# Moving the value loads of a cached attention kernel from SyncE's queue to GpSimd's

## The chip, the cores and the metric

One core of a Trainium2 chip runs the whole program. Its time is the device time of one execution in microseconds (us); the median of two executions before the change is 1309.85 us (1309.16 and 1310.54). The engines named below are PE (TensorE), DVE (VectorE), ACT (ScalarE), POOL (GpSimd) and SP (SyncE). Loads from memory are carried by 16 DMA engines; an engine such as SP or POOL only issues them.

## The reference

Four sequences (B = 4) decode one token each. Attention has 32 heads of width 128 over a cache of 4096 keys and values; beside it stands a gated feed-forward part of width 1792; a gate mixes the two. All data are float32.

```python
def _A_ref(x, k_cache, v_cache, wq, wo):
    q = (x @ wq).reshape(B, Sq, H, Dh).transpose(0, 2, 1, 3)
    scores = jnp.einsum("bhqd,bhkd->bhqk", q, k_cache) * (Dh ** -0.5)
    p = _softmax(scores, axis=-1)
    o = jnp.einsum("bhqk,bhkd->bhqd", p, v_cache)
    return o.transpose(0, 2, 1, 3).reshape(B, Sq, H * Dh) @ wo

def _B_ref(x, w_gate, w_up, w_down):
    return (_gelu(x @ w_gate) * (x @ w_up)) @ w_down

g = _sigmoid((x * gate_w).sum(-1, keepdims=True))
return g * _A_ref(x, k_cache, v_cache, wq, wo) + (1 - g) * _B_ref(x, w_gate, w_up, w_down)
```

The two caches are 268 MB each and are read once. That is nearly all the data that the program moves.

## The kernel before

The work on the caches is cut into NT = 32 tiles: tile i holds the keys (or the values) of four heads of one sequence. In SBUF a tile is 128 partitions by 16384 elements, so 64 KB in each partition and 8.39 MB in all. Partition (h, p) holds 128 consecutive positions of head h.

For tile i, DVE multiplies the keys by the query (`products`, L379) and sums over the head width (`sums`, L385). It does so in two pieces, 32 of the 128 positions first (or last), which it calls shared, then the other 96. Then `soft_max` finds the maximum (L390 to L392), and ACT computes the weights into the one tile PM (L397). PE multiplies the values by the weights (`pv`, L411, 64 matmuls). Each second tile ACT copies the result (`gather_a`, L419), and each fourth tile PE and DVE collect it (`gather`, `weigh`).

One tensor, `big`, holds the large data. It has room for two K tiles which overlap by a quarter (that is why 32 positions of each tile are called shared: their place is needed by the next K tile), and behind them for one V tile. So the load of K tile i + 1 can start once DVE has summed the shared quarter of tile i, and the load of V tile i once PE has finished `pv(i - 1)`. The last V tile goes to the place of K tiles, which is free sooner. The weights use the same space: wq, w_gate and w_up lie in the V place before V tile 0, w_down and wo lie in the K and V places after the tiles that stood there.

The order of the instructions of each engine is the order in which the plan's steps are added in the program; nothing is reordered later. `Plan.add` works out, from the places that a step reads and writes, for which earlier steps it has to wait. Each step counts in a lane, which becomes a semaphore. Compute steps count in their engine's own lane. A load counts in the lane that it names, by 16, and the loads that share a lane have to be in one order. PE, DVE and ACT run the regular turns in a loop over k; the loads aren't in a loop but are written out one by one, each with its wait, in the stream of the issuing engine.

Before the change all loads are issued by SP, through `load` (L255): wq, x, gate_w and K tile 0 at the start, then w_gate and w_up, K tile 1, V tile 0, and from there K and V in turn, at the end w_down and eight pieces of wo. Lanes: "k" for K tiles and also for w_down, "v" for V tiles and for one piece of wo, "vl" for the last V tile, others for the weights. POOL builds the identity matrix at the start (L293, L294) and waits for SP at the very end, to clear the semaphores.

Of the kernel before, what the change touches and what calls it, by code (L numbers as in the profile page):

```python
# [19 lines left out]
class Plan:  # L20
# [18 lines left out]
    def add(self, engine, emit, reads=(), writes=(), lane=None, unit=1):  # L39
        lane = lane or engine  # L40
        self.units[lane] = unit
        row = self.by_lane.setdefault(lane, [])
        step = Step(lane, engine, emit, self.turn if engine in self.loops else None)
        step.at = len(row)
        need = {}
        for accesses, writing in ((reads, False), (writes, True)):
            for name, lo, hi in accesses:
                for other, a, b, wrote in self.past.get(name, ()):
                    if a < hi and lo < b and (wrote or writing):
                        if other.lane == engine and engine == "pe":  # L50
                            continue
                        if other.lane == engine and not wrote:
                            continue
                        need[other.lane] = max(need.get(other.lane, -1), other.at)
        seen = self.seen[engine]
        for l, n in sorted(need.items(), key=lambda x: -len(self.by_lane[x[0]])):
            if seen.get(l, -1) >= n:
                continue
            other = self.by_lane[l][n]
            other.asked = True  # L60
            step.waits[l] = n
            seen[l] = n
            for k, v in self.knew[other].items():
                seen[k] = max(seen.get(k, -1), v)
        step.waits = {l: n for l, n in step.waits.items()
                      if not any(self.knew[self.by_lane[m][k]].get(l, -1) >= n for m, k in step.waits.items() if m != l)}
        self.knew[step] = dict(seen)
        self.knew[step][lane] = step.at
        if row and lane == engine:
            for k, v in self.knew[row[-1]].items():  # L70
                if k != lane:
                    self.knew[step][k] = max(self.knew[step].get(k, -1), v)
        for accesses, writing in ((reads, False), (writes, True)):
            for name, lo, hi in accesses:
                old = self.past.get(name, [])
                if writing:
                    old = [x for x in old if not (lo <= x[1] and x[2] <= hi)]
                self.past[name] = old + [(step, lo, hi, writing)]
        row.append(step)
        self.steps.append(step)  # L80
        return step
# [51 lines left out]
def tile_gated_mix(tc: tile.TileContext, x, kc, vc, wq, wo, w_gate, w_up, w_down, gate_w, out):  # L133
    nc = tc.nc
    P = 128
    B, H, S, D = kc.shape
    DM = x.shape[2]
# [7 lines left out]
    NT = B * NG  # L145
    TW = R * D
# [4 lines left out]
    FC = F // P  # L151
# [15 lines left out]
    def sb(pool, name, shape):  # L167
        sizes[name] = math.prod(shape[1:])
        return pool(name, [P] + list(shape[1:]), F32).ap()[:shape[0]]
# [37 lines left out]
    q = sb(ps, "q", [P, B, D])  # L207
# [6 lines left out]
    Q0, F0, F1, W0, D0 = VA, VA, VA + KC * F, VA, VA + TW // 2  # L214
# [4 lines left out]
    def place(a, n):  # L219
        return big[:, a:a + n]  # L220

    def z(a, n):
        return ("big", a, a + n)
# [15 lines left out]
    add = plan.add  # L239
# [14 lines left out]
    def load(dst, src, writes, lane):  # L254
        return add("sp", lambda: nc.sync.dma_start(dst, src), (), writes, lane=lane, unit=16)  # L255

    def load_kv(kind, i):
        src = (vc, kc)[kind == "k"]
        a = KB_ * (i % 2) if kind == "k" else VA if i < NT - 1 else 0
        s = src[i % B, HT * (i // B):HT * (i // B) + HT].rearrange("h (p r) d -> (h p) (r d)", p=PH)  # L260
        load(place(a, TW), s, [z(a, TW)], "vl" if kind == "v" and i == NT - 1 else kind)

    def KA(i):
        return KB_ * (i % 2)
# [6 lines left out]
             [z((F0, F1)[s], KC * F)], f"f{s}")  # L271

    def load_d():
        load(place(D0, FC * DM), w_down.rearrange("(p i) n -> p (i n)", i=FC), [z(D0, FC * DM)], "k")

    def load_w(w):
        src = wo[w * HW * D:(w + 1) * HW * D].rearrange("(p e) n -> p (e n)", e=E)
        for n, (e0, e1) in enumerate(zip(WO_END[w], WO_END[w][1:])):
            a, m = (W0, W1)[w] + e0 * DM, (e1 - e0) * DM
            lane = (("q",), ("f0", "f1", "g", "v", "x", "w"))[w][n]  # L280
            if (w, e1) == (1, E):
                for lane, b in ((lane, 0), ("e", DM // 2)):
                    load(place(a + b, DM // 2), src[:, e0 * DM + b:e0 * DM + b + DM // 2], [z(a + b, DM // 2)], lane)
            else:
                load(place(a, m), src[:, e0 * DM:e1 * DM], [z(a, m)], lane)

    load(place(Q0, KC * H * D), wq.rearrange("(p c) n -> p (c n)", c=KC), [z(Q0, KC * H * D)], "q")
    load(x_sb, x.rearrange("b s d -> (b s) d"), [z(XS, DM)], "x")
    load(gw, gate_w.rearrange("(s n) -> s n", s=1).to_broadcast([B, DM]), [z(GS, DM)], "g")
    load_kv("k", 0)  # L290
    opening = len(plan.steps)

# [185 lines left out]
    def attended(w, e):  # L478
        a, m = ES + w * E * 32 + e * 32, (W0, W1)[w] + e * DM
        return place(a, 32), place(m, DM), [z(a, 32), z(m, DM)]  # L480
# [55 lines left out]
    for i in range(NT):  # L536
        g, b = divmod(i, B)
# [5 lines left out]
        if i < NT - 1:  # L543
            load_kv("k", i + 1)
        else:
            load_kv("v", i)
# [19 lines left out]
        if i > 0 and b == 0:  # L566
            weigh(g - 1)
    plan.turn = None
    load_d()
    load_w(0)  # L570
    load_w(1)
    expand(0)
    pv(NT - 1)
# [19 lines left out]
    s, w, reads = attended(1, E - 1)  # L593
# [51 lines left out]
```

## Time and profile before

| | |
|---|---|
| median of 2 executions | 1309.85 us |
| the profiled execution's own time | 1309.37 us |
| span of its profile | 1308.0 us |
| moved by DMA | 564.81 MB, mean 432 GB/s |
| busy: DVE | 1155.1 us (88%) |
| busy: PE, weight loads | 352.0 us (27%), 100.0 us (8%) |
| busy: ACT, POOL | 87.3 us (7%), 0.7 us |
| median from issue to landing, K tiles and V tiles | 29.7 us, 29.4 us |

A row of the profile that stands for a group of instructions names line, engine, operation, output and inputs with shapes, how often it occurs, then its busy time, the mean of one, and the idle time of the engine just before, with what ended it. A row of the timeline begins with start and duration in us; in brackets stand the idle time before it and its releaser. A load's row (SPq) shows only the issue on SP; when the data landed is seen from the instruction that waited for it. A row of waits gives the sum, the number and the longest of the waits of one line for one cause. A row of windows gives start and end, length, busy time and number of instructions of PE, weight loads, DVE, ACT and POOL, the clock granted to TensorE, the mean busy share of the DMA engines and GB/s.

### The profile page before, as it was taken

To read this page: it belongs to the slowest core of one execution; us is meant where nothing else is said; L and a number is where in the kernel's file an instruction comes from. 1 tells how busy PE (TensorE), PEld (TensorE's weight loads), DVE (VectorE), ACT (ScalarE), POOL (GpSimd) and SP (SyncE) were. 2 spreads that over 40 slices of the span, in tenths; PEclk is the share of its full clock that TensorE was granted. 3 is DMA by queue.
4 is the path that set the end of the run, shared out by engine and by line. 5 is a ranking of instruction groups with operands and counts; after the bars stand their busy time and mean duration, and the time that the engine had idled before them with its cause. 6 is when DMAs were issued, how large, how long until landed. Compare 5 with 4: busy or idle time off the path is not lost.

```text
span 1308.0 us, 6147 instructions
## 1 busy us (share of the span) xinstructions
PE 352.0 (27%) x2504; PEld 100.0 (8%) x2504; DVE 1155.1 (88%) x299; ACT 87.3 (7%) x291; POOL 0.7 (0%) x6
## 2 busy tenths in 40 slices
PE   2302233202333211322321233321133222122227
PEld 0100001000010000100000000100001000010003
DVE  1899999999899998989989898998989899898991
ACT  0000000000000000000000000000000000000001
POOL 0000000000000000000000000000000000000000
PEclk9656666556666656666656666665667665566669
DMA  9999999999999999999999999999999999999998
GB/s 417 419 443 425 441 441 423 443 429 439 427 441 425 441 427 439 435 433 441 429 439 429 441 425 441 425 441 429 439 439 427 443 429 439 427 441 425 439 428 370
DMA packets 10977, 564.81 MB, mean 432 GB/s; under 512 B 1228, under 2 KB 1484, under 8 KB 1880
## 3 DMA queue, kind: packets, MB, share of 16 engines
q1 hardware_dynamic: 10968, 564.69, 99.7%
q8 instruction: 6, 0.10, 0.0%
q14 instruction: 3, 0.02, 0.0%
HBM read 564.67 MB, written 0.01 MB: 432 GB/s over the span
## 4 chain that ended last, share of the span: by engine, by line
DMA 71%; DVE 28%; issue 1%; PE 0%; SPq 0%; ACT 0%; DVEq 0%; POOLq 0%
DMA big<-in_A_k_cache 69%; DVE big L379 14%; DVE sc L385 13%; DMA big<-in_A_wo 2%; SPq L255 0%; PE acc L493 0%; PE wide L485 0%; DVE hT L525 0%; DVE m L390 0%; DVE big L523 0%; DVE big L522 0%; DVE big L520 0%; ACT big L499 0%; ACT big L521 0%; DVE res L602 0%
## 5 line engine op out<-in xcount | busy, mean ns | idle before, releaser
L379 DVE TENSOR_TENSOR big<-big,qb 128x4096 f32<-128x4096 f32 x64 | 555.9, 8686 | 88.2 <-DMA big<-in_A_k_cache 88.2
L385 DVE TENSOR_REDUCE sc<-big 128x32 f32<-128x4096 f32 x64 | 555.9, 8686 | 2.3
L411 PE MATMUL po<-big,PM 128*32 128x512 f32 x2048 | 293.7, 738 | 902.5 <-DMA big<-in_A_v_cache 902.5
L411 PEld LDWEIGHTS po<-big,PM 128*32 128x32 f32 x2048 | 72.3, 132 | 1117.5 <-DMA big<-in_A_v_cache 826.7
L397 ACT ACTIVATE PM<-sc,nb 32x128 f32<-32x128 f32 x128 | 67.2, 525 | 476.2 <-DVE nb L392 429.5
L419 ACT ACTIVATE o<-po 128x512 f32<-128x512 f32 x16 | 9.6, 597 | 448.7 <-PE po L411 448.7
L397 ACT ACTIVATION_READ_ACCUMULATOR PM<-sc,nb 32x1 f32 x128 | 26.1, 204 | 0.0
L369 ACT ACTIVATE qb<-q 128x512 f32<-128x512 f32 x8 | 4.8, 597 | 247.9 <-PE q L367 247.9
L428 PE MATMUL sm<-o,sel 128*16 128x128 f32 x128 | 15.4, 273 | 5.1 <-ACT o L419 5.1
L312 DVE COPY xT<-sg 128x128 f32<-128x128 f32 x4 | 0.9, 282 | 17.9 <-PE sg L307 17.9
L506 PE MATMUL q<-big,xT 128*32 128x448 f32 x64 | 9.9, 784 | 14.4 <-DMA big<-in_B_w_gate 11.2
L428 PEld LDWEIGHTS sm<-o,sel 128*16 128x16 f32 x128 | 11.7, 97 | 12.8 <-ACT o L419 11.4
L602 DVE COPY res<-acc 4x128 f32<-4x128 f32 x1 | 0.3, 279 | 13.5 <-PE acc L493 13.5
L461 DVE TENSOR_TENSOR tm<-oT,gmask 128x256 f32<-128x256 f32 x2 | 0.8, 424 | 12.6 <-PE oT L455 12.6
L367 PE MATMUL q<-QM,hc 128*128 128x512 f32 x16 | 9.4, 667 | 4.2 <-DVE hc L363 4.2
L390 DVE TENSOR_REDUCE m<-sc 128x1 f32<-128x128 f32 x32 | 9.2, 286 | 1.1
L325 PE MATMUL po<-big,xT 128*32 128x512 f32 x64 | 8.7, 701 | 1.0 <-DVE xT L312 1.0
L391 DVE STREAM_TRANSPOSE mt<-m 128x32 f32<-128x32 f32 x32 | 6.8, 212 | 1.1
L485 PE MATMUL wide<-big 128*32 128x512 f32 x54 | 6.6, 597 | 2.8 <-DMA big<-in_A_wo 2.8
L392 DVE TENSOR_REDUCE nb<-mt 128x1 f32<-128x32 f32 x32 | 5.9, 186 | 1.1
L307 PE MATMUL sg<-ident,big 4*128 4x4 f32 x4 | 0.6, 254 | 23.2 <-DMA big<-in_A_x 23.2
L342 DVE TENSOR_TENSOR big<-po,amask 128x512 f32<-128x512 f32 x2 | 1.3, 684 | 5.9 <-PE po L325 5.9
(72 smaller groups left out, 58.3 us busy)
## 6 DMA issues: line engine op xcount, KB each, us to landing
big<-in_A_wo SPq DMA_DIRECT2D x1, 4096.0 KB, 27.3
big<-in_B_w_gate SPq DMA_DIRECT2D x1, 3584.0 KB, 17.2
big<-in_B_w_up SPq DMA_DIRECT2D x1, 3584.0 KB, 25.4
big<-in_B_w_down SPq DMA_DIRECT2D x1, 3584.0 KB, 18.1
big<-in_A_wo SPq DMA_DIRECT2D x2, 1024.0 KB, 25.8
big<-in_A_wo SPq DMA_DIRECT2D x2, 768.0 KB, 29.5
big<-in_A_k_cache SPq DMA_DIRECT2D x32, 29.7
big<-in_A_v_cache SPq DMA_DIRECT2D x32, 29.4
```

The lines of the kernel that those rows point to most:

```text
L325: last = T.matmul(PO[s][32 * j:32 * j + 32].rearrange("p j d -> p (j d)"), xTf[:, c, :32], w[:, n0:n0 + HB * D], start=c == 0, stop=c == K ...
L367: pe(lambda: T.matmul(q.rearrange("p b d -> p (b d)"), HC.rearrange("p h k -> p (h k)"), QM.rearrange("p b d -> p (b d)"), start=True, sto ...
L379: dve(lambda: V.tensor_tensor(k, k, QB[:, b:b + 1, :].to_broadcast([P, r1 - r0, D]), op=OP.mult), m + t("qb"), m)
L385: dve(lambda: V.tensor_reduce(SC[i % 2][:, r0:r1], k, axis=AX.X, op=OP.add), [z(KA(i) + r0 * D, (r1 - r0) * D)], [(f"sc{i % 2}", r0, r1)])
L390: dve(lambda: V.tensor_reduce(M1[n], SC[n], axis=AX.X, op=OP.max), t(f"sc{n}"), t(f"m1{n}"))
L391: dve(lambda: V.transpose(MT, M1[n].to_broadcast([P, PH])), t(f"m1{n}"), t("mt"))
L397: last = A.activation(PM[:, PZ:].rearrange("p (c m) -> p c m", m=32)[s, :, h:RJ * HT:HT], SC[n][s, :].rearrange("p (c j) -> p c j", j=RJ), ...
L411: last = T.matmul(PO[n][32 * c:32 * c + 32].rearrange("p j d -> p (j d)"), PM[:, m0:m0 + 32], place(VAT(i) + j * N, N), start=b == 0 and j ...
L419: act(lambda: A.activation(O[n], PO[n], AF.Copy), t(f"po{n}"), t(f"o{n}"))
L428: T.matmul(sm[:B * HT, :D], selv[:, j, m0:m0 + B * HT], O[n][:, j, :], start=(n, j) == (0, 0), stop=(n, j) == (N - 1, RJ - 1))
L485: pe(lambda: T.matmul(wide[32 * c:32 * c + 32, :], s, w, start=n < 4, stop=n >= NW - 4), reads, t("wide"))
L506: last = T.matmul(q.rearrange("p b d -> p (b d)")[32 * j:32 * j + 32, :FG], xTf[:, c, :32], place((F0, F1)[s] + c * F + j * FG, FG), start ...
```

## The change

All V tiles are issued by POOL (`nc.gpsimd.dma_start`) in place of SP, in their old order and with the waits that the plan works out for them on POOL. K tiles and all weights remain with SP. Since loads of two issuing engines can't share a lane's count here, w_down moves from lane "k" to a lane "d" of its own, and the piece of wo that counted in "v" counts in a new lane "w2". Places in SBUF, sizes of the loads and the work of all compute engines are as before.

```diff
@@ -258,7 +258,10 @@
         src = (vc, kc)[kind == "k"]
         a = KB_ * (i % 2) if kind == "k" else VA if i < NT - 1 else 0
         s = src[i % B, HT * (i // B):HT * (i // B) + HT].rearrange("h (p r) d -> (h p) (r d)", p=PH)
-        load(place(a, TW), s, [z(a, TW)], "vl" if kind == "v" and i == NT - 1 else kind)
+        if kind == "v":
+            add("pool", lambda: nc.gpsimd.dma_start(place(a, TW), s), (), [z(a, TW)], lane="vl" if i == NT - 1 else "v", unit=16)
+        else:
+            load(place(a, TW), s, [z(a, TW)], kind)
@@ -271,13 +274,13 @@
     def load_d():
-        load(place(D0, FC * DM), w_down.rearrange("(p i) n -> p (i n)", i=FC), [z(D0, FC * DM)], "k")
+        load(place(D0, FC * DM), w_down.rearrange("(p i) n -> p (i n)", i=FC), [z(D0, FC * DM)], "d")
 
     def load_w(w):
...
-            lane = (("q",), ("f0", "f1", "g", "v", "x", "w"))[w][n]
+            lane = (("q",), ("f0", "f1", "g", "w2", "x", "w"))[w][n]
```

## The prediction, made before the changed kernel had run

> **What bounds the kernel now.** First the windows of the trace over the steady part of the loop (length, busy time of PE, weight loads, DVE, ACT, POOL, granted clock, share of the DMA engines, GB/s), then the page's row of DMA queues and the first row of its chain.
>
> ```profile
> 157.04:697.80 540.76, 142.35 (x976) 39.30 (x976) 497.40 (x110) 36.07 (x123) 0.00 (x0) 0.62 1.00 434
> 697.80:1238.76 540.96, 136.56 (x956) 37.37 (x956) 496.53 (x106) 35.47 (x122) 0.00 (x0) 0.63 1.00 434
> q1 hardware_dynamic: 10968, 564.69, 99.7%
> DMA 71%; DVE 28%; issue 1%; PE 0%; SPq 0%; ACT 0%; DVEq 0%; POOLq 0%
> ```
>
> The 16 DMA engines are the bound: share 1.00 at 434 GB/s, one queue filling 99.7% of their span. DVE, at 497.40 of 540.76, is 8% short of being one. 564.69 MB at 434 GB/s are 1301 us of the 1308.0 us span. So the change can win at most about 7 us; it can only lose more.
>
> How does one queue stay full, with two K buffers that overlap and one V buffer? A turn of the loop, from the timeline (start, duration):
>
> ```profile
> 137.67 8.51 PE L411 MATMUL po<-big,PM 128*32 128x512 f32 x64 [29.56 <-DMA big<-in_A_v_cache]
> 146.25 0.33 SPq L255 DMA_DIRECT2D big<-in_A_v_cache  x1
> 157.04 4.42 DVE L379 TENSOR_TENSOR big<-big,qb 128x4096 f32<-128x4096 f32 x1 [2.65 <-DMA big<-in_A_k_cache]
> 161.50 4.42 DVE L385 TENSOR_REDUCE sc<-big 128x32 f32<-128x4096 f32 x1
> 165.94 0.33 SPq L255 DMA_DIRECT2D big<-in_A_k_cache  x1
> 176.35 9.64 PE L411 MATMUL po<-big,PM 128*32 128x512 f32 x64 [30.17 <-DMA big<-in_A_v_cache]
> 186.07 0.33 SPq L255 DMA_DIRECT2D big<-in_A_v_cache  x1
> 214.95 9.12 PE L411 MATMUL po<-big,PM 128*32 128x512 f32 x64 [27.90 <-DMA big<-in_A_v_cache]
> 224.14 0.33 SPq L255 DMA_DIRECT2D big<-in_A_v_cache  x1
> 1209.13 0.33 SPq L255 DMA_DIRECT2D big<-in_A_k_cache  x1
> ```
>
> From the K issue at 165.94 to that at 1209.13 lie 27 turns: 38.64 us each, so a tile of 8.39 MB takes W = 19.32 us. A K tile lands at 157.04, its shared quarter is multiplied and summed, and the next K goes out 8.90 us after the landing. V lands at 137.67, 176.35 and 214.95; the next V goes out 8.58, 9.72 and 9.19 us later, when PE has read the buffer (mean 9.16). Between landing and the next issue a stream asks for nothing: call that its dead time. It is longer for the engines, by what lies between issue and first byte and between last byte and landing. The start prices that:
>
> ```profile
> 0.89 0.39 SPq L255 DMA_DIRECT2D big<-in_A_wq  x1
> 42.33 4.42 DVE L379 TENSOR_TENSOR big<-big,qb 128x4096 f32<-128x4096 f32 x1 [4.80 <-DMA big<-in_A_k_cache]
> ```
>
> wq and the first K, 8.39 MB each, take 42.33 - 0.89 = 41.44 us instead of 38.64: 2.80 us around an idle ring. So K is dead for 11.70 us and V for about 11.96 us. In one ring in order this costs nothing: a dead stream has the other's whole tile, 19.32 us, in front of it, with 7.6 us (K) and 7.4 us (V) to spare.
>
> **The change part by part.** *Semaphores.* The lanes d and w2 add no instruction and no wait; the same steps wait for the same transfers: 0. (V's DMAs can't share a count with another queue's, which is all they are for.)
>
> *The issues.* 32 V issues of 0.33 us leave SP. What does SP wait for?
>
> ```profile
> SPq L255 <- DVE sc L385: 598.1, 32, 22.3
> SPq L255 <- PE po L411: 595.8, 31, 20.2
> DVE big L379 <- DMA big<-in_A_k_cache: 88.2, 30, 4.8
> 3.42 0.20 POOL L293 MEMSET ident<- 128x128 f32 x1 [2.98 <-POOLq L612]
> 3.86 0.29 POOL L294 TENSOR_SCALAR_AFFINE_SELECT ident<-ident 128x128 f32<-128x128 f32 x1 [0.23 <-POOL ident L293]
> 4.26 0.54 DVE L299 TENSOR_REDUCE sel<-ident 128x8 f32<-128x32 f32 x4 [0.46 <-POOL ident L294]
> ```
>
> It waits nearly all the time, and each issue follows its own event within 0.1 us (165.94 after 161.50 + 4.42); no K issue is held by a V wait. Removing them wins 0. On POOL only the two ident instructions stand ahead of them, done at 4.2 us, and behind the last V only the closing clear of semaphores; after 4.2 us no engine waits for POOL. What POOL needs beyond SP's issue, d, no row shows. The lower end is 0 (SP's own 0.33 is inside the 2.80). The upper end is 12.95 us, if descriptor work on POOL had to stand behind one of DVE's long instructions (L379 and L385 at 12288 elements). I take 1.0, from the nearest rows: POOL's two instructions and DVE's wake-up behind them, 0.20 + 0.29 + 0.46. V's dead time becomes 11.96 + d = 12.96 us. [...]
>
> *Two rings.* This is the core. Two queues no longer keep K, V, K, V in order: while both have work, each engine serves both. Total work is the same, so the time grows exactly by the time in which both streams are dead together, which one ring in order never had. How finely the engines alternate decides. The page's packets bear on it:
>
> ```profile
> DMA packets 10977, 564.81 MB, mean 432 GB/s; under 512 B 1228, under 2 KB 1484, under 8 KB 1880
> ```
>
> 10977 - 1880 = 9097 large packets carry the 564.7 MB, 62 KB each: the 64 KB row of one partition. They fill 99.7% of 16 engines without overlap, so an engine moves one row at a time; a tile is 8 rows per engine, 19.32 / 8 = 2.415 us each. I take it that two rings alternate row by row.
>
> Then a cycle of 16 rows exists in which the streams lock. V ends; K is alone for 5 rows (12.08 us) while V is dead. V restarts and is alone while K is dead (11.70 us, rounded up to the end of a row: 5 rows). Then 3 rows each in turn; V ends. K has had 5 + 3 rows, V 5 + 3. A shift of less than a row is swallowed by the row in service, except where V's dead time exceeds 5 rows: that excess is idle DMA. With d = 1.0 and the three V gaps, dead times are 12.38, 13.52 and 12.99, less 12.08: 0.30, 1.44, 0.91, mean 0.89 us a turn. Of the turns about 28 are in this state: 25 us. (With d = 0.4: 0.39 a turn, 11 us; with d = 0, 0.15 a turn, 4 us; at 1.5, 1.38 a turn, 39 us. Above some 2 us the excess nears a row, the lock breaks and the drift of the rivals starts.)
>
> *Head.* The first V now shares with the second K:
>
> ```profile
> 59.37 4.55 PE L506 MATMUL q<-big,xT 128*32 128x448 f32 x32 [3.13 <-DMA big<-in_B_w_up]
> 69.66 0.33 SPq L255 DMA_DIRECT2D big<-in_A_v_cache  x1
> 83.44 4.42 DVE L379 TENSOR_TENSOR big<-big,qb 128x4096 f32<-128x4096 f32 x1
> ```
>
> K1 would land at 59.37 + 19.32 = 78.7. V0 joins at 69.66 + 2.80 + 1.0 = 73.5, with 5.2 us of K1 left, so K1 lands near 84 and DVE, which wants it at 83.44, loses under 1 us; its 88.2 us of waiting in 30 turns cover that: 0. V0 then has 14 us left.
>
> *Tail.* V31 no longer stands ahead of w_down and wo; it shares with them from 1268 on.
>
> ```profile
> 1267.98 0.33 SPq L255 DMA_DIRECT2D big<-in_B_w_down  x1
> 1277.72 8.51 PE L411 MATMUL po<-big,PM 128*32 128x512 f32 x64 [9.80 <-DMA big<-in_A_v_cache]
> 1292.88 0.32 ACT L476 ACTIVATE big<-t 128x160 f32<-128x160 f32 x1
> 1295.84 4.50 PE L485 MATMUL wide<-big 128*32 128x512 f32 x40 [1.60 <-DMA big<-in_A_wo]
> 1302.64 1.06 PE L485 MATMUL wide<-big 128*32 128x512 f32 x6 [0.76 <-DMA big<-in_A_wo]
> ```
>
> The 6.9 us of V31 left at 1270.8 (1268 + 2.8) stretch to twice that. From its landing the chain to the last operand is 15.5 us (1277.72 to 1293.2), now ending near 1300; 54 matmuls (4.50 + 1.06 + 1.06) then end near 1307 instead of 1303.7. That is 0 to 5 us; I take 3.
>
> *Sum*, on the profiled execution's 1309.37: + 0 + 25 + 0 + 3 = 1337.4. That execution is 0.5 under the median 1309.85, so the forecast for a median is **1338**.
>
> **The rivals.**
>
> *Tiles stay whole.* An engine finishes what it began of one DMA before it turns to the other ring, or the rings are served in order of arrival. Then K, V, K, V stays, d eats 1.0 of the 7.4 us V has to spare, and the time is 1309 to 1313 (tail included). For it: rows of one tile do run back to back. Against it: within one ring they must. Also if the V issues ended up in the same ring, this is the result. [...]
>
> *Fine sharing, drift.* If the rings share below a row, nothing locks. Each turn K gains the difference of the dead times, 12.96 - 11.70 = 1.3 us, on V. At K's landing V has 14 us left at first; once that reaches 18.0 (19.32 - 1.3), 3 turns on, both dead times begin to overlap, by 1.3 us more each turn up to 11.7 after 9 turns (58 us lost), then less for another 9 (53 us). About + 111: 1420; with d = 0.2 it starts at turn 10 and still loses some 100.
>
> *V's rows in one packet, K's row by row.* V then always goes first. From a K landing (118.87), weights are ready at 156.6:
>
> ```profile
> 118.87 4.42 DVE L379 TENSOR_TENSOR big<-big,qb 128x4096 f32<-128x4096 f32 x1
> 156.37 0.20 ACT L397 ACTIVATION_READ_ACCUMULATOR PM<-sc,nb 32x1 f32 x1
> ```
>
> 37.7, + 9.2 for PE, + 3.8 to V's first byte: 50.7 after that landing. In a turn of P, V starts 50.7 - P after the next K landing, runs 19.32, then K 19.32: P = 50.7 - P + 38.64 = 44.7. Against 38.64 over 29 turns: + 175, 1485.
>
> *V's rows cut smaller than K's.* Turn by turn K gets more, runs ahead until the weights can't overwrite PM before PE has read it, and then both wait at V's landing: 12.96 + 38.64 = 51.6 a turn. From about the eighth turn on, + 13 on some 22 turns: near 1600.
>
> *Held issues*, d near 12.95: V alone needs 24.9 + 19.32 = 44.2 a turn, + 5.6 on 30 turns at least, 1478 and up; I give it no chance apart from the last case.
>
> **How the numbers follow.** Row by row with a lock 0.38 (1312 to 1360 by d from 0 to 2); whole tiles 0.17; drift 0.22; V first 0.10; small V rows or held issues 0.11; a win of some us or something else 0.02. The range from 1308 to 1495 leaves out the 0.11, half of V first and the odd rest. About 2% (26 us) is what a measurement of this kernel tells from no change. Faster by more than that 0.01: there are 7 us to win. Within: whole tiles 0.17, half of the lock (d below 1) 0.20, odd 0.01, together 0.38. Slower 0.61.
>
> **What would show it.** In the changed profile: a second large queue with 268 MB; K's time from issue to landing other than 29.7; GB/s of the steady windows at 424 (38.64 / 39.5), evenly over the slices; K and V landings at a fixed distance near 5 or 11 rows. A GB/s row that sags and recovers means drift; a uniform 375 V first; 434 throughout whole tiles. My number is wrong if rows aren't the unit of alternation, or if POOL needs more than 2 us for an issue.

## The result, and the profile after

The changed kernel takes **1355.74 us** (median of 1355.36 and 1356.13), the kernel before 1309.85: a ratio of 1.0353 (95% interval 1.0336 to 1.037), slower by 46 us. The forecast was 1338, the range 1308 to 1495.

The page of the changed kernel: span, packets, the two large queues, the chain, DVE's wait for K, POOL's issues, and the medians from issue to landing.

```profile
span 1353.8 us, 6147 instructions
GB/s 403 434 434 434 432 432 425 415 405 403 434 403 426 411 432 405 434 403 434 426 405 409 434 432 411 397 434 434 420 430 418 405 403 403 411 426 432 405 421 339
DMA packets 10976, 564.80 MB, mean 417 GB/s; under 512 B 1228, under 2 KB 1484, under 8 KB 1880
q1 hardware_dynamic: 6360, 296.25, 51.9%
q0 software_dynamic: 4608, 268.44, 45.8%
DMA 77%; DVE 21%; PE 2%; issue 0%; SPq 0%; ACT 0%; DVEq 0%; POOLq 0%
L382 DVE TENSOR_TENSOR big<-big,qb 128x4096 f32<-128x4096 f32 x64 | 556.0, 8687 | 136.3 <-DMA big<-in_A_k_cache 136.3
L262 POOL DMA_DIRECT2D big<-in_A_v_cache x32 | 17.0, 532 | 1276.5 <-PE po L414 1185.0
big<-in_A_k_cache SPq DMA_DIRECT2D x32, 31.1
big<-in_A_v_cache POOLq DMA_DIRECT2D x32, 30.5
```

The same bytes move in the same number of packets, but in two queues. DVE's instructions last as long as before; DVE waits 136.3 us for K where it had waited 88.2. And GB/s is not evenly lower, as it would be with a fixed loss a turn: slices at the full 434 stand beside slices near 403.

The windows over the steady part and over the tail of the changed kernel:

```profile
165.09:687.62 522.53, 132.23 (x894) 35.60 (x894) 461.42 (x101) 33.36 (x114) 6.86 (x13) 0.61 0.98 419
687.62:1209.68 522.06, 132.49 (x910) 36.73 (x910) 461.83 (x102) 33.36 (x114) 6.86 (x13) 0.62 0.98 418
1287.93:1353.80 65.87, 32.91 (x308) 12.49 (x308) 41.13 (x22) 5.19 (x15) 0.53 (x1) 0.75 0.89 375
```

Before, they showed share 1.00 and 434 GB/s. Now the DMA engines stand still for 2% of the time, and 419 and 418 GB/s are more than 2% below 434: some of their busy time is slow, too. The first turns in the timeline (start, duration; DVE's row starts at K's landing, PE's at V's):

```profile
69.83 0.67 POOL L262 DMA_DIRECT2D big<-in_A_v_cache  x1 [65.68 <-DVE hT L528]
86.68 4.43 DVE L382 TENSOR_TENSOR big<-big,qb 128x4096 f32<-128x4096 f32 x1 [3.27 <-DMA big<-in_A_k_cache]
98.77 8.48 PE L414 MATMUL po<-big,PM 128*32 128x512 f32 x64 [36.39 <-DMA big<-in_A_v_cache]
107.61 0.53 POOL L262 DMA_DIRECT2D big<-in_A_v_cache  x1 [37.11 <-PE po L414]
125.47 4.42 DVE L382 TENSOR_TENSOR big<-big,qb 128x4096 f32<-128x4096 f32 x1 [3.27 <-DMA big<-in_A_k_cache]
137.56 9.56 PE L414 MATMUL po<-big,PM 128*32 128x512 f32 x64 [30.31 <-DMA big<-in_A_v_cache]
147.46 0.53 POOL L262 DMA_DIRECT2D big<-in_A_v_cache  x1 [39.33 <-PE po L414]
```

V lands 98.77 - 86.68 = 12.09 us after K, and 137.56 - 125.47 = 12.09 in the next turn: five rows of 2.418. POOL issues V 0.34 us after PE's last matmul (147.46 - 137.56 - 9.56), where SP had needed 0.07 (146.25 - 137.67 - 8.51, in the prediction's rows).

Where do the 46 us arise? K1 is multiplied at 86.68 instead of 83.44: **+3.2**. From there to K31, 30 turns, before takes 1155.3 us (83.44 to 1238.76) and after 1201.25 (86.68 to 1287.93): **+45.9**. From K31 to the end before takes 69.2, after 65.87: **-3.4**, since the last V but one has less left to bring. Sum 45.8, and the spans differ by 1353.8 - 1308.0 = 45.8.

All 30 turns of the changed kernel, sorted by how many rows V landed behind K at the turn's beginning and at its end (worked out from the timeline's rows of L382 and L414; V was always within 0.4 us of 4 or 5 whole rows):

```
V behind K   turns   mean length   beyond 38.64   in all
5 -> 5        11       39.20          +0.56        + 6.2
5 -> 4         5       42.78          +4.14        +20.7
4 -> 4         9       40.53          +1.89        +17.0
4 -> 5         5       38.26          -0.38        - 1.9
                                                   +42.0
```

The forecast's lock exists, at 5 rows. But there is a second one, at 4 rows, and 14 of 31 landings of V fall on it. A turn there is 1.9 us longer, and the one that leads there 4.1; most of the 4.1 is K's landing moving by a row against V's, as the records of the DMA engines will show.

What the DMA engines do in such turns shows in the packet records of the trace (start, duration, size and queue of each packet). They don't name the engine; a row that begins where another ended is taken to be on the same one, which leaves open who is who after a gap, but not how long the gaps are in all. Three of the 16 engines of the changed kernel from 205 us on (K: a 64 KB row of keys, V: of values; in brackets idle time in us):

```
205.0 VVVVKKKKKKKVKVVVVVVVKKKKKKKVKVVVVVVV(2.7)KK
205.4 VVVVKKKKKKKVKVVVVVVVKKKKKKVKVKVVVVVV(2.5)KK
206.1 VVVVKKKKKKVKVKVV(0.3)VVVVKKKKKKVKVKVVVVVV(1.7)KK
```

An engine serves one row at a time, and where both queues have work it alternates, K, V, K, V. That is the forecast's rule of row by row. What is different: only one to three rows of each are shared, and the idle time stands **after V**, when K isn't back yet. From 165 to 1205 us an engine before carries 430 rows with 0.1 us between them. After, it carries 415, stands idle for about 22 us, nearly all between a V and a K, and spends another 16 us on rows that last longer, most of them the first after a gap (3.1 us in place of 2.42). Together 38 us, about the time of the 15 rows that are missing. The median row lasts 2.418 us as before, so a second queue doesn't stretch the rows as such.

From K1 to K31 idle time and longer rows come to 42.6 us an engine, beside the 42.0 of the table. The 14 turns that begin with V at 4 rows have 31.6 of it (2.3 each), the 16 that begin at 5 rows 11.0 (0.7 each).

The records also show the completion of a load: a packet of 4 bytes in its queue behind the last row of each engine. For K tiles 1 to 30 that makes 480; 466 of them come directly behind a row of V, the rest behind another packet of 4 bytes, none behind a row of K. DVE gets K 0.3 to 0.5 us after the last of them. Before, it got K 0.3 to 0.5 us after K's last row (from K3 on).

### The profile page after: what moved, and what is told of

It reads as the page before. It is cut to its first block, busy times and chain, and to the rows that moved or that the text cites. A ratio compares the mean times of both kernels' runs of the same rounds, so it can differ in the third digit from the quotient of the medians.

```text
span 1353.8 us, 6147 instructions
## 1 busy us (share of the span) xinstructions
PE 355.4 (26%) x2504; PEld 100.8 (7%) x2504; DVE 1155.3 (85%) x299; ACT 87.3 (6%) x291; POOL 17.7 (1%) x38
## 3 DMA queue, kind: packets, MB, share of 16 engines
q0 software_dynamic: 4608, 268.44, 45.8%
## 4 chain that ended last, share of the span: by engine, by line
DMA 77%; DVE 21%; PE 2%; issue 0%; SPq 0%; ACT 0%; DVEq 0%; POOLq 0%
DMA big<-in_A_k_cache 75%; DVE big L382 10%; DVE sc L388 10%; DMA big<-in_A_v_cache 2%; PE po L414 1%; PE wide L488 1%; PE oT L458 0%; PE acc L496 0%; DVE big L451 0%; SPq L255 0%; DVE big L444 0%; ACT big L502 0%; DVE res L605 0%; DVE tm L464 0%; DVE t L466 0%
## 5 line engine op out<-in xcount | busy, mean ns | idle before, releaser
L382 DVE TENSOR_TENSOR big<-big,qb 128x4096 f32<-128x4096 f32 x64 | 556.0, 8687 | 136.3 <-DMA big<-in_A_k_cache 136.3
L414 PE MATMUL po<-big,PM 128*32 128x512 f32 x2048 | 298.3, 748 | 948.6 <-DMA big<-in_A_v_cache 948.6
L414 PEld LDWEIGHTS po<-big,PM 128*32 128x32 f32 x2048 | 73.1, 134 | 1167.5 <-DMA big<-in_A_v_cache 860.5
L262 POOL DMA_DIRECT2D big<-in_A_v_cache x32 | 17.0, 532 | 1276.5 <-PE po L414 1185.0
L431 PEld LDWEIGHTS sm<-o,sel 128*16 128x16 f32 x128 | 11.7, 97 | 12.8 <-ACT o L422 11.4
L464 DVE TENSOR_TENSOR tm<-oT,gmask 128x256 f32<-128x256 f32 x2 | 0.8, 424 | 12.6 <-PE oT L458 12.6
## 6 DMA issues: line engine op xcount, KB each, us to landing
big<-in_B_w_down SPq DMA_DIRECT2D x1, 3584.0 KB, 21.7
big<-in_A_k_cache SPq DMA_DIRECT2D x32, 31.1
```

The costliest lines, as they stand in the source:

```text
L262: add("pool", lambda: nc.gpsimd.dma_start(place(a, TW), s), (), [z(a, TW)], lane="vl" if i == NT - 1 else "v", unit=16)
L382: dve(lambda: V.tensor_tensor(k, k, QB[:, b:b + 1, :].to_broadcast([P, r1 - r0, D]), op=OP.mult), m + t("qb"), m)
L414: last = T.matmul(PO[n][32 * c:32 * c + 32].rearrange("p j d -> p (j d)"), PM[:, m0:m0 + 32], place(VAT(i) + j * N, N), start=b == 0 and j ...
L431: T.matmul(sm[:B * HT, :D], selv[:, j, m0:m0 + B * HT], O[n][:, j, :], start=(n, j) == (0, 0), stop=(n, j) == (N - 1, RJ - 1))
```

## Experiments

Four questions: is it the second queue at all, and which kind of queue? Does the software queue itself cost anything? Which dead time makes the idle time? What decides between 4 and 5 rows? The diffs of e1, e2 and e3 are against the kernel before (e3's without its new lanes), the others against the changed kernel; all are shortened. The kernel before took 1309.3 to 1309.6 us beside each of them.

**e1, the lanes alone.** All loads on SP; only the lanes are the changed kernel's.

```diff
-        load(place(D0, FC * DM), ..., [z(D0, FC * DM)], "k")
+        load(place(D0, FC * DM), ..., [z(D0, FC * DM)], "d")
-            lane = (("q",), ("f0", "f1", "g", "v", "x", "w"))[w][n]
+            lane = (("q",), ("f0", "f1", "g", "w2", "x", "w"))[w][n]
```

> Only the two semaphore lanes are new; all loads are issued by SP as before. Theory (two rings alternating row by row, so that K and V come to be dead together): one ring, so the time of the kernel before, 1309 to 1311. Rival that the lanes carry the loss: 1350 and more.

1309.35 us, ratio 0.9999 (0.9989 to 1.0008). The windows show the kernel before:

```profile
157.00:1238.00 1081.00, 279.75 (x1932) 76.92 (x1932) 993.97 (x216) 71.11 (x244) 0.00 (x0) 0.62 1.00 434
```

The semaphores cost nothing. All the loss comes with V's queue.

**e2, every load on POOL.** One queue as before, but the software one.

```diff
-        return add("sp", lambda: nc.sync.dma_start(dst, src), (), writes, lane=lane, unit=16)
+        return add("pool", lambda: nc.gpsimd.dma_start(dst, src), (), writes, lane=lane, unit=16)
```

> Every load, weights too, is issued by POOL in the old order, so there is one ring again, but the software-issued one. Theory: the order K, V, K, V is back, each stream has about 7 us to spare, and the slower issue of POOL (first row 3.6 us after the issue in the changed kernel's packets, against 1.0 us for SP) shows only at the start and the end: 1312 to 1316. Rival that each transfer issued by POOL costs some 1.5 us by itself: 32 such transfers cost 46 us, 64 and the weights about 95, so 1355 to 1405.

1328.05 us, 1.014 (1.0123 to 1.0157): 12 us over what was expected. The windows of the steady part, and one row of the start:

```profile
180.00:1100.00 920.00, 239.65 (x1656) 65.30 (x1656) 847.47 (x185) 59.67 (x204) 25.31 (x48) 0.62 1.00 434
44.18 0.20 POOL L293 MEMSET ident<- 128x128 f32 x1 [40.44 <-POOLq L612]
```

The steady part is that of before: 434 GB/s, and 27 turns of 38.66 us (213.87 to 1257.71 by the rows of L379). All the extra time is at the start. POOL, which now issues the opening loads, gets to the identity matrix (L293) at 44.18 us where it had been at 3.42, and the other engines wait for that. What holds it is a wait that the program has there, the line L612 that closes its opening section: the trace has a DRAIN of POOL at L612 from 3.09 us on, for 40.41 us. K0's last row ends at 43.00. Before, with no load of POOL's on its way, this DRAIN took 0.04 us.

**e5, the same without that start.** K from its second tile on and V on POOL, the opening loads and the weights on SP.

```diff
+        if kind == "v" or i:
+            add("pool", lambda: nc.gpsimd.dma_start(place(a, TW), s), (), [z(a, TW)], lane=..., unit=16)
+        else:
+            load(place(a, TW), s, [z(a, TW)], "k0")
```

> K tiles from the second on and all V tiles are issued by POOL, the opening loads and the weights by SP. In the run with every load on POOL the turns took 38.63 us, as before the change, and its 18 us were lost at the start, where all engines waited 44 us for the opening loads. Theory (time is lost where both streams are dead together, which one ring in order prevents): 1311 to 1316. Rival that a second ring or the software issue costs by itself: 1330 and more.

1316.6 us, 1.0055 (1.0038 to 1.0072). DVE's wait for K in the page, its last K tiles in the timeline, and the queues:

```profile
L382 DVE TENSOR_TENSOR big<-big,qb 128x4096 f32<-128x4096 f32 x64 | 556.0, 8687 | 86.9 <-DMA big<-in_A_k_cache 86.9
1207.01 4.43 DVE L382 TENSOR_TENSOR big<-big,qb 128x4096 f32<-128x4096 f32 x1 [3.29 <-DMA big<-in_A_k_cache]
1245.62 4.42 DVE L382 TENSOR_TENSOR big<-big,qb 128x4096 f32<-128x4096 f32 x1 [3.02 <-DMA big<-in_A_k_cache]
q0 software_dynamic: 9072, 528.49, 92.8%
```

A turn takes 38.61 us, and DVE's wait is back at 86.9. V lands 8.0 rows after K in every turn but the first two: whole tiles alternate. The 7 us lie at the head, where the weights' queue and K's are two (K31 at 1245.62 instead of 1238.76). So the software queue was no slower here than SP's, 38.61 us a turn against 38.64, with K and V both in it.

**e3, V in ACT's queue.** Two queues again, both hardware ones.

```diff
-        load(place(a, TW), s, [z(a, TW)], "vl" if kind == "v" and i == NT - 1 else kind)
+        if kind == "v":
+            ...
+                return nc.scalar.dma_start(place(a, TW), src2)
+            ...
+        else:
+            load(place(a, TW), s, [z(a, TW)], kind)
```

> V tiles are issued by ACT, in ACT's own ring, at the same places of the order; no load comes from POOL. It tells the second ring from the software issue. Theory: V's dead time falls from 9.2 + 0.3 + 3.6 + 1.6 = 14.7 us to 9.2 + 0.1 + 1.0 + 1.6 = 11.9, under 5 rows, while K's stays at 8.9 + 1.0 + 1.6 = 11.5 plus up to one row of 2.4 that its completion waits behind a V row: mostly no common dead time, 1312 to 1330. Rival that a second ring costs as such, because rows are stretched (2.46 against 2.42 us): 1345 to 1356. Rival that software issue is the whole cause: 1309 to 1312.

1357.03 us, 1.0354 (1.0337 to 1.0371): a miss, and the most telling one. Its queues and a window:

```profile
q1 hardware_dynamic: 6360, 296.25, 51.7%
q10 hardware_dynamic: 4608, 268.44, 45.6%
330.64:734.89 404.25, 101.50 (x700) 28.31 (x700) 355.39 (x79) 25.85 (x88) 0.00 (x0) 0.62 0.97 415
```

Without POOL the loss is the same. V lands 5 rows behind K at first and in 19 of 31 turns 4; ten turns in 404.25 us are 40.4 each. So it isn't POOL's slowness, the forecast's d, that the time is lost to, but a second queue. d itself can be read from the packet records: on an idle engine the first row begins 1.23 us after POOL's issue (e4, e8) and 0.96 us after SP's or ACT's; with 0.27 us more from PE's end to the issue, d is 0.5 us, half of what I had taken.

**e4, V back sooner.** Half of the value matmuls left out.

```diff
-            for j in range(m):
+            for j in [*range(m // 4), *range(m - m // 4, m)]:
```

> The changed kernel with half of the 64 matmuls of the values left out (the values of half of the positions are loaded but not weighed), so that PE frees the V place some 4.6 us sooner. Theory: V's dead time falls from 14.7 to 10.1 us, about 4 rows; the common dead time of the turns shrinks, 1310 to 1330. Rivals that the second ring or the POOL issue costs as such: the loss does not depend on PE, 1350 to 1356.

1456.25 us, 1.1142 (1.1107 to 1.1177): the theory that the idle time is V's dead time beyond 5 rows falls. K and V in the second and the fifth turn, and a wait:

```profile
128.14 4.42 DVE L382 TENSOR_TENSOR big<-big,qb 128x4096 f32<-128x4096 f32 x1 [5.87 <-DMA big<-in_A_k_cache]
137.93 5.75 PE L414 MATMUL po<-big,PM 128*32 128x512 f32 x32 [32.56 <-DMA big<-in_A_v_cache]
...
265.76 4.42 DVE L382 TENSOR_TENSOR big<-big,qb 128x4096 f32<-128x4096 f32 x1 [11.40 <-DMA big<-in_A_k_cache]
268.19 5.48 PE L414 MATMUL po<-big,PM 128*32 128x512 f32 x32 [36.78 <-DMA big<-in_A_v_cache]
...
PE po L414 <- ACT PM L400: 757.0, 21, 38.5
```

V lands 12.1, 9.8, 7.3, 4.9 and 2.4 us behind K: 5, 4, 3, 2, 1 rows, one less a turn. With each row the DMA engines wait longer for K (DVE's wait goes from 5.87 to 11.40 us), until V is there before its weights, and PE waits for ACT. By the packet records an engine is idle for 12.9 us between a V and a K up to 268 us, and from then on for 88 us between a K and a V, since V now waits for its weights. Sooner is worse: in the first turns because K is what the engines wait for, and behind them because V is held up by the weights.

**e7, K back sooner.** The shared quarter's product and sum over half of the head width.

```diff
+        h = D // 2 if shared else D
-        dve(lambda: V.tensor_tensor(k, k, QB[:, b:b + 1, :]..., op=OP.mult),
+        dve(lambda: V.tensor_tensor(k[:, :, :h], k[:, :, :h], QB[:, b:b + 1, :h]..., op=OP.mult),
```

> The changed kernel with only the shared quarter's product and sum cut to half of the head width: K's dead time falls from 14.1 to about 9.7 us, V's stays at 14.7. Theory: a difference of 5 us, two rows a turn, the other way round than with half of the matmuls; K runs ahead, both streams come to be dead together within some five turns, 1400 to 1480. Rival that shorter dead times are better: 1310 to 1340.

1528.25 us, 1.1672 (1.1648 to 1.1695), more than the 1400 to 1480. K runs ahead: V lands 7, 11 and 15 rows behind it in the first turns.

**e6, both sooner**, e4's and e7's edits together.

> The changed kernel with half of the values' matmuls left out, and half of the head width left out in the shared quarter's product and sum: both dead times are shorter, V's by 4.6 us to about 10.1, K's by 4.4 us to about 9.7 with the row that its completion waits. Theory as it stands after the run with half of the matmuls (the DIFFERENCE of the two dead times makes the streams drift against each other until they are dead together; their length alone does not): the difference is 0.4 to 0.6 us as in the changed kernel, the streams hold their distance for long, 1312 to 1356. Rival that V is hurt by coming back early (it then waits for its weights): 1450, as with half of the matmuls.

1405.72 us, 1.0736 (1.0695 to 1.0777): missed. Equal cuts don't keep the balance. V is 5, 7, 9 and 11 rows behind K in the first turns, K's turns are 36.2 us, 15 rows; then every group of four turns takes some 167 us in place of 154.6.

**e8, the queues exchanged**: K from POOL, V from SP.

```diff
-        if kind == "v":
+        if kind == "k":
```

> K tiles from POOL, V tiles from SP. Theory: K's dead time grows by the slower first row and the later issue to about 17 us, V's falls to 11.9: difference 5 us, two rows a turn, V runs ahead until it waits for its weights, 1400 to 1480. Rival that it matters only that there are two rings: 1350 to 1360, as with V from POOL or from ACT.

1398.94 us, 1.0684 (1.0659 to 1.0709). The number lies 1 us below the expected range, but the reason given for it is wrong: nothing drifts. Two turns of the timeline:

```profile
630.28 4.42 DVE L382 TENSOR_TENSOR big<-big,qb 128x4096 f32<-128x4096 f32 x1 [5.29 <-DMA big<-in_A_k_cache]
639.97 9.56 PE L414 MATMUL po<-big,PM 128*32 128x512 f32 x64 [31.34 <-DMA big<-in_A_v_cache]
671.15 4.42 DVE L382 TENSOR_TENSOR big<-big,qb 128x4096 f32<-128x4096 f32 x1 [5.35 <-DMA big<-in_A_k_cache]
680.78 9.64 PE L414 MATMUL po<-big,PM 128*32 128x512 f32 x64 [31.25 <-DMA big<-in_A_v_cache]
```

V stays 4 rows behind K (9.69 and 9.63 us). This turn takes 40.87 us, and the 24 that begin and end at 4 rows 41.06 on average: 0.53 more than the 40.53 of the changed kernel's own turns at 4 rows. Now POOL's longer issue is on K, 0.54 us by the figures under e3, and K is what the engines wait for. The span is 40.9 us longer than the changed kernel's: 17.2 come from the start, as in e2 (K1 at 103.88 in place of 86.68), and 23.6 from 30 turns of 40.83 us on average in place of 40.04, where V, once at 4 rows, never gets back to 5.

**e9 and e10, V back later.** 16 or 8 further matmuls behind those of each tile, their result thrown away. They were to take about 2.4 or 1.2 us; in the traces V's next issue comes 12.9 and 11.5 us after its landing, where it is 9.7 in the changed kernel, so it was 3.2 and 1.8.

```diff
+            for j in range(16):          # 8 in e10
+                c = j % 4
+                last = T.matmul(wide[32 * c:32 * c + 32, :], PM[:, PZ:PZ + 32], place(VAT(i) + j * N, N), start=True, stop=True)
```

> The changed kernel with 16 matmuls more behind the 64 of each V tile, their results thrown away, so that PE frees the V place about 2.4 us (one row) LATER. Theory after the first eight runs (what is lost in a turn is K's dead time, 2.86 + 8.9 + 0.96 = 12.7 us by the packets, less the V rows that are left when K ends, 4 or 5 rows of 2.42 in the slow turns): a V that comes back a row later has had a row less beside K and has one more left to cover K's dead time, so the kernel with more work gets faster, 1312 to 1335. Rival, the sum of the prediction (V's own dead time is what is in excess): 2.4 us more in 28 turns, 1400 to 1425. Rival that neither counts: 1356.

> The same with 8 matmuls more, about 1.2 us, half a row. Theory: fewer turns fall into the state with 4 rows left, 1320 to 1352. The prediction's sum: 1375 to 1395. Neither counts: 1356.

e9 took 1490 to 1525 us in four executions, e10 1438.6 us, 1.0992 (1.0942 to 1.1042). So my second theory, that a later V spares the engines the wait for K, falls as well. e10's first turns and one of its waits:

```profile
86.79 4.42 DVE L382 TENSOR_TENSOR big<-big,qb 128x4096 f32<-128x4096 f32 x1 [3.24 <-DMA big<-in_A_k_cache]
98.87 9.05 PE L414 MATMUL po<-big,PM 128*32 128x512 f32 x64 [35.06 <-DMA big<-in_A_v_cache]
...
123.31 4.43 DVE L382 TENSOR_TENSOR big<-big,qb 128x4096 f32<-128x4096 f32 x1 [1.01 <-DMA big<-in_A_k_cache]
140.62 8.65 PE L414 MATMUL po<-big,PM 128*32 128x512 f32 x64 [30.99 <-DMA big<-in_A_v_cache]
...
159.91 4.42 DVE L382 TENSOR_TENSOR big<-big,qb 128x4096 f32<-128x4096 f32 x1 [1.07 <-DMA big<-in_A_k_cache]
181.63 8.63 PE L414 MATMUL po<-big,PM 128*32 128x512 f32 x64 [30.64 <-DMA big<-in_A_v_cache]
...
366.53 4.42 DVE L382 TENSOR_TENSOR big<-big,qb 128x4096 f32<-128x4096 f32 x1 [13.06 <-ACT qb L372]
```

V's turn is 140.62 - 98.87 = 41.75 and then 41.01 us, 17 rows; K's is 36.52 and 36.60, 15 rows. So V falls behind by two rows a turn: 12.1, 17.3, 21.7 us. Here there is next to no idle time yet (0.1 us an engine), since the two turns together are still 32 rows. The loss begins when K can run ahead no further: each fourth tile needs a new query (qb), which PE makes only behind the value matmuls of an earlier tile. That is the last row, 13.06 us of waiting. From then on the turns repeat in fours (38, 41, 49 and 45 us).

**e11, both loads in halves.** Each K and V load becomes two of half the columns, so rows of 32 KB.

```diff
+        N = 2
+        for n in range(N):
+            m = TW // N
+            dst, src2, w = place(a + n * m, m), s[:, n * m:n * m + m], [z(a + n * m, m)]
+            ...
```

> The changed kernel with each K and V tile loaded by two transfers of half the width, so that a row of a partition is 32 KB and 1.21 us. Theory (the engines alternate by rows and have one row in hand): V lands a multiple of 1.21 us behind K, half rows included; K's completion waits 1.21 us instead of 2.42, and a newcomer's first row on a busy engine comes after some 2.2 to 2.6 us instead of 3.6 to 4. V comes back earlier against K, K's dead time is 11.5 us: the streams need not hold, 1330 to 1450. Rival that the engines alternate by something else than rows (whole tiles, fixed time slices): distances stay at 9.67 and 12.09 us, 1356.

1350.7 us, 1.0316 (1.0295 to 1.0337). V lands 10.91, 12.14, 14.65, 16.98, 19.46, 21.82, 24.18 us behind K (each of the last three twice): steps of about 1.21 and 2.42 us, and the first distance is no multiple of 2.42. Landings alone would be thin evidence, but the packet records show rows of 1.213 us that alternate one by one (KVKVKVKV) in the stretches that K and V share. The row was the unit at both sizes, 64 and 32 KB. Here no lock holds the two together: K runs ahead from the first turns, at 37.5 to 38.8 us a turn, until the query stops it here too. The twelfth K tile in the timeline:

```profile
512.05 4.42 DVE L388 TENSOR_TENSOR big<-big,qb 128x4096 f32<-128x4096 f32 x1 [7.12 <-ACT qb L378]
```

The time in all is about that of the changed kernel.

**e12, V back a little sooner.** Eight of the 64 value matmuls left out.

```diff
-            for j in range(m):
+            for j in [*range(m * 7 // 16), *range(m - m * 7 // 16, m)]:
```

> The changed kernel with 8 of the 64 value matmuls of each tile left out (its output lacks an eighth of the products with the values): PE's part of V's dead time becomes 7.4 to 8.7 us instead of 8.4 to 10.0, about 1.1 us less, under half a row. Theory (turn by turn a threshold decides): in the trace of the changed kernel, with V landing 4 rows (9.67 us) after K, the next V went back to 5 rows only when PE's matmuls had taken 9.63 us or more; with PE always under that, V should stay at 4 rows from about the third turn on, each turn 40.4 to 40.6 us, K31 multiplied from about 1300 us, and the time 1358 to 1372; if it slips further, 3 rows and fewer, 1380 and more, as with half of the matmuls. Rival (what is less than a row is swallowed, as the prediction had it): the mix of 5 and 4 rows stays, 1350 to 1357. Rival (the idle time is V's dead time beyond 5 rows, so a shorter one is cheaper): 5 rows throughout, turns of 38.7 to 39.6, 1315 to 1345.

This one was written with the turns of the changed kernel in view: from 4 rows V had gone back to 5 only where PE's matmuls ended 19.29 to 19.41 us after K's landing (and one at 19.29 had not), so with shorter matmuls it never should. (The 9.63 us of the expectation, for PE alone, leave out one V that went back after 9.47 us of matmuls, having landed at 9.82.) The four executions scatter: 1327, 1348, 1369 and 1370 us, at granted clocks of 0.615 to 0.621. They give no verdict on the time. The only trace is of the one that took 1370:

```profile
333.20 4.42 DVE L382 TENSOR_TENSOR big<-big,qb 128x4096 f32<-128x4096 f32 x1 [4.96 <-DMA big<-in_A_k_cache]
342.85 9.12 PE L414 MATMUL po<-big,PM 128*32 128x512 f32 x56 [31.59 <-DMA big<-in_A_v_cache]
...
373.54 4.43 DVE L382 TENSOR_TENSOR big<-big,qb 128x4096 f32<-128x4096 f32 x1 [4.82 <-DMA big<-in_A_k_cache]
383.21 7.72 PE L414 MATMUL po<-big,PM 128*32 128x512 f32 x56 [30.19 <-DMA big<-in_A_v_cache]
...
333.20:697.58 364.38, 82.91 (x546) 22.18 (x546) 319.42 (x70) 23.15 (x79) 4.77 (x9) 0.60 0.97 414
```

V stands 9.65 and 9.67 us behind K, and from the second tile on always within 0.4 us of 4 rows, while PE's time goes from 7.65 to 9.17 us (V is issued again 0.9 us sooner than in the changed kernel); nine turns in 364.38 us are 40.49 each. That is the theory's case, with its time, in this one execution. The execution of 1327 us can't have been in it: 30 turns at 1.9 us are 57 us. It left no trace, so what it did instead, and what settles it, no run here shows.

## Why the prediction was right, and where it was wrong

**Bound and upper limit: right.** The kernel was bound by the DMA engines, and nothing was to be won.

**Lanes and issues at 0: right** (e1; and in e5 the issues are on POOL at no cost in the steady part).

**Direction right, size in part luck.** The time lies in the range, and the cost of two queues that alternate by rows is idle DMA engines, as forecast. But with the d that the runs show, the forecast's own sum would have been some 1326 (13 us in place of 25). That 28 forecast and 46 measured are as near as they are rests on a d taken too large.

**Rows alternate one by one: right.** The packet records show it, e11 shows it for another size of row, and the landings at 5 whole rows were forecast. Where both queues had work an engine switched after each 64 KB row, so the tiles did not stay whole, and the time is not that rival's 1309 to 1313. The second issuing engine bought no bandwidth: 419 and 418 GB/s in the changed kernel's windows and 415 in e3's, against 434 before, and both kernels took 3.5% longer.

**The excess of V's dead time over 5 rows, 0.89 us a turn and 25 us: the step that failed.** The turns lost 42 us against 38.64 each, 45.9 against the turns of before, and for another reason. Three things in it were wrong.

- *d was 0.5, not 1.0 us* (1.23 - 0.96 + 0.27 = 0.54), and V's dead time isn't what the engines wait for. The 1.0 in the sum was an estimate and no run shows it, nor any of its trial values (0, 0.4, 1.5) for POOL. By the forecast's own line for d, 0.5 would have been some 13 us; ACT's queue, with a smaller d, lost as much, and e4 shows that a shorter dead time of V is no cheaper. (So does the traced execution of e12; the one of 1327 us speaks against, and stays unexplained.)
- *An engine acts as if it had one row in hand.* On busy engines the first of the 16 begins a V tile 3.6 to 5.4 us after POOL's issue (up to 3.9 in 19 of 30 turns), against 1.23 on idle ones. The earliest is the idle figure plus a row, 1.23 + 2.42 = 3.65, and so it is with ACT (3.37 against 0.96 + 2.42) and SP (3.35, K in e4): the newcomer lets the row in service end and one more of the other queue. K's completion, too, waits for a V row: K's last row ends 2.72 to 2.91 us before DVE gets K. The one ring at the start, from which I had my 2.80 us around an idle ring, could not show that. K's dead time for the engines is 2.78 + 8.90 + 0.96 = 12.6 us (2.78 the mean) and not 11.70, which is 5.2 rows: more than the 5 into which the forecast had "rounded up" it.
- *So the idle time stands at the mirrored place.* In a turn at 4 rows V's last row ends 9.67 - 0.35 = 9.3 us after K's landing (0.35: from the last row to the landing with nothing between), and K's first row can't begin before 8.90 + 0.96 = 9.86. That is 0.5 us of gap on the engine that has V last, and more on those that have done with V before it: by the packet records an engine is idle for 1.6 us in a turn that begins and ends at 4 rows, and its rows take 0.7 us longer. In a turn at 5 rows V's last row ends at 11.7, and K is back by then: 0.1 us idle and 0.4 of longer rows, the + 0.56 of the table.

**"A shift of less than a row is swallowed": too hopeful.** The lock is hardly wider than the spread of PE's own time, 8.4 to 10.0 us. 1.8 us more (e10) gave V a turn of 17 rows and K one of 15; 0.9 us less (e12, the traced execution) put it at 4 rows. The rival "fine sharing, drift" had the right picture of what comes then, but drift doesn't need sharing below a row. Here whole rows did it: the turns of V and K differed by one row in e4 and by two in e10.

What takes the changed kernel from 5 rows to 4 stays open. PE's time alone doesn't decide it: V fell to 4 rows after matmuls of 8.46 to 9.37 us, and stayed at 5 after matmuls of 8.48 to 10.03. That it is the 16 engines getting out of step is likely from their differing sequences, and not shown.

**Head at 0 and tail at +3: off by a few us.** They were +3.2 and -3.4; the stretched V31 was right in itself, but V30 was further on when K31 landed.

**What would show it.** The second queue with 268 MB came, K's issue to landing moved from 29.7 to 31.1, the landings are at whole rows. GB/s was to be 424 evenly: it is 419 and 418, unevenly, and that already spoke against one fixed loss a turn.

No kernel here beats the one before; the lanes without the queue (e1) equal it.

## What to carry to other kernels

Of two load streams that wait for each other's consumers, as here, keep both in one queue, in the order of their need: a stream's dead time then hides behind the other's whole tile, with 7 us to spare here (7.6 for K, 7.4 for V, by the forecast's estimate), and neither POOL's slower issue nor its software queue cost anything in the steady part (e2: 434 GB/s and 38.66 us a turn; e5: 38.61; before: 38.64). With the streams split over two queues, the engines alternated row by row, and the streams kept their distance only where both turns came out at the same number of rows, dead time included (e10: 17 rows for V, 15 for K, and V fell behind by 5.2 and 4.4 us in two turns). In a kernel like this one reckon with a row in hand (a newcomer's first row after 3.6 us, not 1.23) and with a completion behind the other's row (2.72 to 2.91 us, not 0.3 to 0.5), and expect a lock that one or two microseconds of compute time can break (1.8 more in e10, 0.9 less in the traced execution of e12).

## What the runs showed of the hardware that I had not expected

- A load that joined engines busy with another queue got its first row about a whole row, 2.42 us, later than on idle engines: after 3.6 us at the earliest (POOL) or 3.4 (ACT, SP), against 1.23 (POOL) and 0.96 (SP, ACT).
- A K tile's completion came behind a row of the other queue, in 466 of 480 cases directly: K was there for DVE 2.72 to 2.91 us after its last row, against 0.3 to 0.5 with one queue in the steady part.
- The first row after a gap took 3.1 us on average in the changed kernel, not 2.42.
- A second hardware queue (ACT's) cost as much as the software one: 1.0354 against 1.0353.
- A DRAIN of POOL with its own loads on their way lasted 40.4 us in e2 and 40.0 in e8, until they were in, against 0.04 with none.
- Executions of one program differed by 3%: e12 took 1327 to 1370 us at granted clocks of 0.615 to 0.621, where all executions of the kernel before lie within 1.5. Why is not shown; the one that was traced stood in the lock at 4 rows.
